# The channel MLP's beta as an extra matmul column and a relu bias, with the first batch's loads in another order

## The chip, the cores and the metric

The kernel runs on one core of a Trainium2 chip. The metric is the time of one execution in microseconds of the device (us); the time before is the median of 11 runs. Beside it there is one profiled execution, from which all durations below come.

## The reference

Grouped attention over 8 batches is followed by an MLP block over tokens and channels, with affine scalings in place of normalisations:

```python
# q: (8, 16, 384, 64), k and v: (8, 4, 384, 64); each K/V head serves 4 Q heads
scores = q @ k.T / 8
attn = softmax(scores) @ v                 # per head
x = attn.transpose(0, 2, 1, 3).reshape(8, 384, 1024)

a1 = alpha1 * x + beta1
tok = einsum('ts,bsd->btd', w_tok, a1)     # mixes tokens, w_tok: (384, 384)
u = x + lam * tok
a2 = alpha2 * u + beta2
ch = maximum(a2 @ w_ch1, 0) @ w_ch2        # w_ch1: (1024, 4096), w_ch2: (4096, 1024)
out = u + lam * ch
```

Inputs and output are float32. The kernel multiplies in bfloat16 and adds in float32.

## The kernel before, in words

The work of a batch has two parts. `side(b)` is a list of small units that make the attention and the token mixing of batch b, and end in `a2T`, the transposed input of the channel MLP. `main(b)` is the channel MLP of batch b. The program does `side(0)` alone, and then for each b runs `main(b)` with the units of `side(b + 1)` put between its matmuls at an even pace. The order on every engine is the order in which the program is written (`manual_schedule`): no engine takes a later instruction ahead of a waiting one.

`side(b)` goes by pairs of heads, p = 0 to 7, of 128 channels each. K and Q are transposed on TensorE for the first two batches (`k_transpose`, `q_transpose`, a group of two pairs each, through one PSUM buffer `tp`) and by DMA later. `scores(p, sk)` makes two matmuls and one ScalarE exp, `av_piece(p, hh)` the attention's values for one head of the pair. When the second head is done, VectorE divides by the softmax's sum (lines 207 and 210), multiplies by `g1`, which holds alpha1 times lam (L213, `a1f`), and `h1` (beta1 times lam) is added (L216): on GpSimd in the first batch for p < 6, and on VectorE otherwise. `tok(p)` mixes tokens by nine matmuls (L223, one PSUM buffer in batch 0), adds x (L226), multiplies by `al2` (L228, `a2f`) and adds `be2` (L231), again on GpSimd for p < 6 of batch 0. `a2_transpose(p)` brings a2 into `a2T`, in batch 0 by DMA from the SP queue for p < 5 and by TensorE and ScalarE for the last three. There are three buffers of a2, so that pair 7 takes that of pair 4 after its transpose has landed.

`main(b)` first runs 32 blocks of eight matmuls against W1 (L327, 384 columns each), with two PSUM buffers `mm` in turn. ScalarE takes relu of the even blocks (L332), VectorE that of the odd ones (L334). W1 does not stay in SBUF: a tile of 512 KB (two blocks) is loaded for each of 16 chunks in every batch, from GpSimd's queue, which also casts to bfloat16, into a ring of `RING = 4` buffers. A new load is issued after the matmuls that free its buffer. Then come six blocks of 32 matmuls against W2 (L347), which is loaded once, in pieces, during batch 0.

The loads of the first batch are issued ahead of `side(0)`. SP's queue carries K of batches 0 and 1 (`load_k`, two halves each, two buffers `kst`) and the broadcasts of `g1`, `lam`, `h1` (columns from 256 on), `al2` and `be2`; ScalarE's queue carries the Q of the first four heads and the broadcasts of columns 0 to 255; GpSimd's queue carries the rest of Q, V (three loads), `w_tok`, four W1 tiles, and, at places of the unit list that the table `loads` gives, half of W2 and then Q and V of batch 1. `place_k(b, i)` casts a half of K, one copy on VectorE and one on ScalarE. The pair of heads 2 and 3 (`place_k(0, 1)`) is cast ahead of the units, and its transposes stand in pair 1.

Of the kernel before, what the change touches and what calls it, by code (L numbers as in the profile page):

```python
# [12 lines left out]
def kernel(  # L13
# [21 lines left out]
    nc = tc.nc  # L35
    f32 = mybir.dt.float32
# [19 lines left out]
    NCH = NNT // CW  # L56
    RING = 4
    scale_qk = 1.0 / float(D) ** 0.5
# [9 lines left out]
    hT = const.tile([P, NNT, S], bf, tag="hT", name="hT")  # L68
    g1, h1, lam_t, al2, be2 = (const.tile([P, DM], f32, tag=n, name=n)
                               for n in ("g1", "h1", "lam", "al2", "be2"))  # L70
    kT = const.tile([P, NST, Hkv, P], bf, tag="kT", name="kT")
# [16 lines left out]
    def place_k(b, i):  # L88
        if i == 0:
            k2s[b] = sb.tile([P, NST, Hkv, 2, D], bf, tag="k2", name="k2", bufs=1)  # L90
        copies = (nc.vector.tensor_copy, nc.scalar.copy) if b < 2 else [nc.gpsimd.tensor_copy] * 2
        for a in range(2):
            copies[a](out=k2s[b][:, :, 2 * i:2 * i + 2, a, :], in_=ks[b][i].rearrange("p h st d -> p st h d"))
# [41 lines left out]

    xs, a2Ts = {}, {}

    def side(b):
        vb = vt[b % 2]
        x = sb.tile([P, NST, DM], f32, tag="x", name="x", bufs=2)  # L140
        xs[b] = x
        a2Ts[b] = sb.tile([P, NDT, S], bf, tag="a2T", name="a2T", bufs=2)
        ess, avs, a1s, a2s = {}, {}, {}, {}
# [74 lines left out]
        def tok(p):  # L218
            ps = psum.tile([P, NST, P], f32, tag="av" if first else "sc", name="tok",
                           bufs=1 if first else 2)  # L220
            for tt in range(NST):
                for st in range(NST):
                    nc.tensor.matmul(out=ps[:, tt, :], lhsT=wtokT[:, st, tt * P:(tt + 1) * P],  # L223
                                     rhs=a1s[p][:, st, :], start=(st == 0), stop=(st == NST - 1))
            u = x[:, :, cols(p)]
            nc.vector.tensor_tensor(out=u, in0=ps, in1=u, op=ADD)  # L226
            t = sb.tile([P, NST, P], f32, tag="tmp", name="a2f", bufs=4)
            nc.vector.tensor_tensor(out=t, in0=u, in1=bc(al2, p), op=MUL)  # L228
            a2s[p] = sb.tile([P, NST, P], bf, tag="a2", name="a2", bufs=3)
            eng = nc.gpsimd if first and p < NP - 2 else nc.vector  # L230
            eng.tensor_tensor(out=a2s[p], in0=t, in1=bc(be2, p), op=ADD)  # L231

        def a2_transpose(p):
            if not pe_flip or first and p < NP - 3:
                nc.sync.dma_start_transpose(
                    out=a2Ts[b][:, p, :].rearrange("p (a s) -> p a s", a=NST),
                    in_=a2s[p].rearrange("p a d -> p (a d)"))
                return
            ps = tp_ps([P, NST, P])
            for tt in range(NST):  # L240
                nc.tensor.matmul(out=ps[:, tt, :], lhsT=a2s[p][:, tt, :], rhs=ident,
                                 is_transpose=True, start=(tt == 0), stop=(tt == NST - 1),
                                 skip_group_check=True)
            nc.scalar.copy(out=a2Ts[b][:, p, :], in_=ps.rearrange("p a b -> p (a b)"))

# [44 lines left out]
        for p in range(NP):  # L290
            add(scores, p, 0)
            if p == 1:
                add(k_transpose, 2)
            add(scores, p, 1)
            if p < 3:
                add(q_transpose, p + 1)
            if p > 0:
                add(av_piece, p - 1, 0)
            if p == 2:
                add(wtok_transpose)  # L300
            if p > 2:
                add(tok_flip if p < NP - 1 else tok, p - 3)
            add(scores, p, 2)
            if p > 0:
                add(av_piece, p - 1, 1)
        for p in range(NP - 3, NP):
            if p == NP - 2:
                add(av_piece, NP - 1, 0)
                add(av_piece, NP - 1, 1)
            add(tok, p)  # L310
        for p in range(NP - 4, NP):
            add(a2_transpose, p)
        return us
# [4 lines left out]
    def main(b):  # L318
        a2T = a2Ts.pop(b)
        x = xs.pop(b)  # L320
        for c in range(NCH):
            w1 = w1_tiles.pop(b * NCH + c)
            for j in range(CW):
                nt = c * CW + j
                ps = psum.tile([P, 512], f32, tag="mm", name="h", bufs=2)
                for dt in range(NDT):
                    nc.tensor.matmul(out=ps[:, :S], lhsT=w1[:, dt, j * P:(j + 1) * P],  # L327
                                     rhs=a2T[:, dt, :], start=(dt == 0), stop=(dt == NDT - 1))
                    if dt == 3:
                        yield T_H  # L330
                if nt % 2 == 0:
                    nc.scalar.activation(out=hT[:, nt, :], in_=ps[:, :S], func=RELU)  # L332
                else:
                    nc.vector.tensor_scalar_max(out=hT[:, nt, :], in0=ps[:, :S], scalar1=0.0)  # L334
                yield T_H
# [24 lines left out]
    with tc.manual_schedule(engines=order):  # L360
# [6 lines left out]
        load_k(0)  # L367
        qst = sb.tile([P, NST, DM], f32, tag="x", name="qst", bufs=2)
        qst = qst[:, 0, :G * NST * D].rearrange("p (h st d) -> p h st d", h=G, st=NST)
        nc.scalar.dma_start(out=qst, in_=q[0, :G].rearrange("h (p st) d -> p h st d", st=NST))  # L370
        load_q(0, range(1), G)
        make_identity(nc, ident)
        for t in vt:
            nc.vector.memset(t[:, :, :, D:], 1.0)
        load_q(0, range(1, NST), G)
# [78 lines left out]
```

The softmax here doesn't subtract the row's maximum and nothing guards it: scores larger than these inputs give would overflow.

## Time and the profile before

| | us |
|---|---|
| median of 11 runs (lowest, highest) | 837.83 (834.91, 841.7) |
| profiled execution, its own time | 840.0 |
| span of the profile | 838.2 |
| TensorE busy (share of the span) | 805.5 (96%) |
| VectorE busy | 372.2 (44%) |
| ScalarE busy | 213.2 (25%) |
| GpSimd busy | 195.5 (23%) |
| W1 matmuls L327, 2048 of 327 ns | 362.4 |
| W2 matmuls L347, 1485 of 379 ns | 346.3 |
| first W1 matmul starts at | 54.59 |
| first W2 matmul starts at | 114.32 |
| batch 7's W1 part starts at | 746.66 |

Matmuls are pipelined, so the time of one is longer than the distance to the next: eight W1 matmuls take about 1.31 us when they follow each other. The page gives busy time by engine and by 40 slices of the span; the timeline gives each engine's instructions in order, and in brackets the idle time ahead of one with what ended it. "DMA q_raw<-in_q_dram" there means that the engine waited for that load. The chain of waits follows the work that ended last back from the end of the program.

### The profile page before, as it was taken

How to read it: one execution, taken by the hardware profiler on the slowest of the kernel's cores; microseconds unless marked ns; L12 is line 12 of the kernel's file. 1: busy time of each engine (PE TensorE's matmuls, PEld its weight loads, DVE VectorE, ACT ScalarE, POOL GpSimd, SP SyncE). 2: the span in 40 equal slices, each digit the busy share in tenths (PEclk: the TensorE clock that was granted, in tenths of full speed). 3: DMA queues.
4: the chain of work that ended last, by engine and by line, in shares of the span. 5: the costliest groups of instructions: out<-in, count | busy, mean ns of one | idle time of the engine just before them, and what ended most of it. 6: DMA issues, size and time to landing. Idle time of an engine off the chain costs nothing.

```text
span 838.2 us, 13671 instructions
## 1 busy us (share of the span) xinstructions
PE 805.5 (96%) x5768; PEld 436.7 (52%) x5819; DVE 372.2 (44%) x751; ACT 213.2 (25%) x337; POOL 195.5 (23%) x237
## 2 busy tenths in 40 slices
PE   5769999999999999999999999999999999999997
PEld 3545654455455654556545564556545565455443
DVE  3864653145463435534454453534455344542111
ACT  3515420232203332043212332033320432101100
POOL 5624451023301250022400223012500221003000
PEclk9979999999999999999999999999999999999999
DMA  9999999799948999499917999489994999139711
GB/s 215 214 109 173 200 204 200 141 171 179 117 90 137 173 180 79 96 170 176 155 47 147 166 179 124 89 129 171 183 86 97 144 180 124 35 70 179 101 38 38
DMA packets 265501, 115.39 MB, mean 138 GB/s; under 512 B 114272, under 2 KB 258528, under 8 KB 265440
## 3 DMA queue, kind: packets, MB, share of 16 engines
q0 software_dynamic: 202416, 83.47, 88.4%
q1 hardware_dynamic: 62064, 30.26, 15.7%
q10 hardware_dynamic: 960, 0.79, 0.4%
q8 instruction: 45, 0.74, 0.3%
q14 instruction: 16, 0.13, 0.0%
HBM read 173.08 MB, written 12.58 MB: 221 GB/s over the span
## 4 chain that ended last, share of the span: by engine, by line
PE 90%; DMA 3%; DVE 3%; issue 2%; POOL 1%; ACT 1%; DVEq 0%; POOLq 0%; ACTq 0%
PE ch L347 40%; PE h L327 38%; PE sc L179 4%; PE av L197 4%; PE tok L223 3%; DMA v<-in_v_dram 1%; DMA w<-in_moe_w_ch_dram 1%; DMA a2T<-a 1%; DVE a2f L228 1%; POOL w L125 1%; DVE x L210 0%; DVE a1f L213 0%; ACT hT L332 0%; DVE x L226 0%; PE tp L167 0%
## 5 line engine op out<-in xcount | busy, mean ns | idle before, releaser
L327 PE MATMUL h<-a2T,w 128*128 128x384 bf16 x2048 | 362.4, 327 | 3.5 <-DMA w<-in_moe_w_ch_dram 2.7
L347 PE MATMUL ch<-w,hT 128*128 128x512 bf16 x1485 | 346.3, 379 | 2.7
L327 PEld LDWEIGHTS <-w 128*128 128x128 bf16 x2048 | 190.0, 98 | 138.0 <-issue 20.4
L125 POOL DMA_DIRECT2D w<-in_moe_w_ch_dram x128 | 112.4, 879 | 558.3 <-PE sc L179 274.3
L347 PEld LDWEIGHTS <-hT 128*128 128x128 bf16 x1536 | 143.1, 98 | 162.0 <-issue 7.6
L182 ACT ACTIVATE es<-sc 128x768 bf16<-128x768 f32 x192 | 145.2, 808 | 318.8 <-PE sc L179 318.8
L334 DVE TENSOR_SCALAR hT<-h 128x384 bf16<-128x384 f32 x128 | 71.1, 555 | 165.3 <-PE h L327 165.2
L332 ACT ACTIVATE hT<-h 128x384 bf16<-128x384 f32 x128 | 62.9, 492 | 211.9 <-PE h L327 211.9
L352 DVE TENSOR_TENSOR o<-ch,lam 128x512 f32<-128x512 f32 x48 | 33.1, 689 | 127.0 <-PE ch L347 127.0
L226 DVE TENSOR_TENSOR x<-tok,x 128x384 f32<-128x384 f32 x64 | 35.6, 556 | 84.1 <-PE tok L223 84.1
L197 PEld LDWEIGHTS <-es 128*128 128x128 bf16 x1152 | 52.6, 99 | 25.5 <-issue 5.5
L197 PE MATMUL av<-v,es 128*128 128x65 bf16 x1152 | 57.7, 196 | 2.6 <-DMA v<-in_v_dram 2.6
L179 PE MATMUL sc<-qT,kT 64*128 64x384 bf16 x384 | 51.6, 340 | 1.6 <-ACT es L182 0.9
L223 PE MATMUL tok<-a,wtokT 128*128 128x128 bf16 x576 | 44.1, 223 | 9.0 <-DVE x L226 5.1
L223 PEld LDWEIGHTS <-wtokT 128*128 128x128 bf16 x576 | 38.5, 100 | 20.6 <-issue 7.9
L210 DVE TENSOR_TENSOR x<-av,rinv 128x192 f32<-128x192 f32 x128 | 39.8, 352 | 2.2
L228 DVE TENSOR_TENSOR a2f<-x,al 128x384 f32<-128x384 f32 x64 | 38.2, 598 | 2.6
L213 DVE TENSOR_TENSOR a1f<-x,g 128x384 f32<-128x384 f32 x64 | 37.6, 587 | 2.6
L207 DVE RECIPROCAL rinv<-av 128x6 f32<-128x6 f32 x64 | 12.2, 191 | 55.5 <-PE av L197 55.5
L353 DVE TENSOR_TENSOR o<-o,x 128x512 f32<-128x512 f32 x48 | 33.2, 692 | 1.6
L231 DVE TENSOR_TENSOR a<-a2f,be 128x384 bf16<-128x384 f32 x58 | 32.3, 558 | 2.8 <-DMA a2T<-a 0.8
L216 DVE TENSOR_TENSOR a<-a1f,h 128x384 bf16<-128x384 f32 x58 | 32.5, 561 | 2.0
(37 smaller groups left out, 147.8 us busy)
## 6 DMA issues: line engine op xcount, KB each, us to landing
w<-in_moe_w_ch_dram POOLq DMA_DIRECT2D x135, 512.0 KB, 6.6
out_dram<-o SPq DMA_DIRECT2D x48, 256.0 KB, 2.1
q_raw<-in_q_dram POOLq DMA_DIRECT2D x21, 256.0 KB, 8.9
kst<-in_k_dram SPq DMA_DIRECT2D x16, 192.0 KB, 3.0
w<-in_moe_w_ch_dram POOLq DMA_DIRECT2D x10, 256.0 KB, 8.9
w<-in_moe_w_ch_dram POOLq DMA_DIRECT2D x1, 2048.0 KB, 32.7
v<-in_v_dram POOLq DMA_DIRECT2D x24, 64.0 KB, 8.8
a2T<-a SPq DMA_TRANSPOSE x53, 5.1
```

The lines of the kernel that those rows point to most:

```text
L125: nc.gpsimd.dma_start(out=t, in_=w1src[:, :, c * CW * P:(c + 1) * CW * P])
L179: nc.tensor.matmul(out=sc[:, hh, :S].rearrange("p (st s) -> p st s", st=NST), lhsT=kT[r, sk, hk, :], rhs=qT[r, :, p, :], start=True, stop= ...
L182: nc.scalar.activation(out=e, in_=sc[:, :, :S], func=EXP, scale=scale_qk)
L197: nc.tensor.matmul(out=av[:, hh, sq, :], lhsT=ess[p, sk][:, hh, sq * P:(sq + 1) * P], rhs=vb[:, sk, hk, :], start=(sk == 0), stop=(sk == N ...
L210: nc.vector.tensor_tensor(out=x[:, :, c0:c0 + D], in0=av[:, hh, :, :D], in1=rinv[:, hh].to_broadcast([P, NST, D]), op=MUL)
L213: nc.vector.tensor_tensor(out=t, in0=x[:, :, cols(p)], in1=bc(g1, p), op=MUL)
L223: nc.tensor.matmul(out=ps[:, tt, :], lhsT=wtokT[:, st, tt * P:(tt + 1) * P], rhs=a1s[p][:, st, :], start=(st == 0), stop=(st == NST - 1))
L228: nc.vector.tensor_tensor(out=t, in0=u, in1=bc(al2, p), op=MUL)
L327: nc.tensor.matmul(out=ps[:, :S], lhsT=w1[:, dt, j * P:(j + 1) * P], rhs=a2T[:, dt, :], start=(dt == 0), stop=(dt == NDT - 1))
L332: nc.scalar.activation(out=hT[:, nt, :], in_=ps[:, :S], func=RELU)
L334: nc.vector.tensor_scalar_max(out=hT[:, nt, :], in0=ps[:, :S], scalar1=0.0)
L347: nc.tensor.matmul(out=ps, lhsT=hT[:, nt, ms * P:(ms + 1) * P], rhs=w2[:, nt, cs], start=(nt == 0), stop=(nt == NNT - 1))
```

## The change

Four things are changed.

1. The addition of beta2 goes. a2 is now alpha2 times u alone, one VectorE instruction. Since W1 is linear, the missing term is one number for each of W1's 4096 columns, the product of beta2 and W1. It comes as a 385th column of the right side in batch 0's W1 matmuls: beta2 is loaded as 128 x 8 single numbers and copied into column 384 of `a2T`. After each of the 32 blocks of batch 0 VectorE copies that column's result to `bias1`, and relu takes it as a bias, in all batches. `a2T` becomes two fixed tiles, and `w_tok` is loaded into a part of the tile `stage` that x uses later.
2. The loads of batch 0 are in another order. V comes as float32 from SP's queue, behind the first two halves of K, and GpSimd casts it. K of batch 1 stands ahead of the broadcasts. The broadcast of beta2 is gone.
3. In the unit list `k_transpose(2)` and `q_transpose(1)` to `(3)` stand one pair later, `place_k(0, 1)` is done after the first three scores with both copies on VectorE, and at the end the last a2 transposes stand between the last tok units. Loads of W2 and of batch 1's Q and V stand at other places of the list.
4. `RING` is 5.

```diff
-    RING = 4
+    RING = 5
...
+    bias1 = const.tile([P, NNT], f32, tag="bias1", name="bias1")
+    a2Ts = [const.tile([P, NDT, S + 16 * (1 - i)], bf, tag=f"a2T{i}", name=f"a2T{i}") for i in range(2)]
...
-        copies = (nc.vector.tensor_copy, nc.scalar.copy) if b < 2 else [nc.gpsimd.tensor_copy] * 2
+        copies = (nc.vector.tensor_copy, nc.vector.tensor_copy if i else nc.scalar.copy) if b < 2 else [nc.gpsimd.tensor_copy] * 2
...
-            t = sb.tile([P, NST, P], f32, tag="tmp", name="a2f", bufs=4)
-            nc.vector.tensor_tensor(out=t, in0=u, in1=bc(al2, p), op=MUL)
             a2s[p] = sb.tile([P, NST, P], bf, tag="a2", name="a2", bufs=3)
-            eng = nc.gpsimd if first and p < NP - 2 else nc.vector
-            eng.tensor_tensor(out=a2s[p], in0=t, in1=bc(be2, p), op=ADD)
+            nc.vector.tensor_tensor(out=a2s[p], in0=u, in1=bc(al2, p), op=MUL)
...
             add(scores, p, 0)
-            if p == 1:
+            if p == 2:
                 add(k_transpose, 2)
             add(scores, p, 1)
-            if p < 3:
-                add(q_transpose, p + 1)
+            if 0 < p < 4:
+                add(q_transpose, p)
...
-        for p in range(NP - 3, NP):
-            if p == NP - 2:
-                add(av_piece, NP - 1, 0)
-                add(av_piece, NP - 1, 1)
-            add(tok, p)
-        for p in range(NP - 4, NP):
-            add(a2_transpose, p)
+        add(tok, NP - 3)
+        add(a2_transpose, NP - 4)
+        add(av_piece, NP - 1, 0)
+        add(av_piece, NP - 1, 1)
+        add(tok, NP - 2)
+        add(a2_transpose, NP - 3)
+        add(tok, NP - 1)
+        add(a2_transpose, NP - 2)
+        add(a2_transpose, NP - 1)
...
+        n = S + 1 if b == 0 else S
...
-                    nc.tensor.matmul(out=ps[:, :S], lhsT=w1[:, dt, j * P:(j + 1) * P],
-                                     rhs=a2T[:, dt, :], start=(dt == 0), stop=(dt == NDT - 1))
+                    nc.tensor.matmul(out=ps[:, :n], lhsT=w1[:, dt, j * P:(j + 1) * P],
+                                     rhs=a2T[:, dt, :n], start=(dt == 0), stop=(dt == NDT - 1))
...
+                c1 = bias1[:, nt:nt + 1]
+                if b == 0:
+                    nc.vector.tensor_copy(out=c1, in_=ps[:, S:n])
                 if nt % 2 == 0:
-                    nc.scalar.activation(out=hT[:, nt, :], in_=ps[:, :S], func=RELU)
+                    nc.scalar.activation(out=hT[:, nt, :], in_=ps[:, :S], func=RELU, bias=c1)
                 else:
-                    nc.vector.tensor_scalar_max(out=hT[:, nt, :], in0=ps[:, :S], scalar1=0.0)
+                    nc.vector.tensor_scalar(out=hT[:, nt, :], in0=ps[:, :S], scalar1=c1,
+                                            scalar2=0.0, op0=ADD, op1=mybir.AluOpType.max)
...
+        vst = stage[:, 2, :Hkv * NST * D].rearrange("p (h st d) -> p h st d", h=Hkv, st=NST)
+        nc.sync.dma_start(out=vst, in_=v[0].rearrange("h (p st) d -> p h st d", st=NST))
+        nc.gpsimd.tensor_copy(out=vt[0][:, :, :, :D], in_=vst.rearrange("p h st d -> p st h d"))
         place_k(0, 0)
...
+        load_k(1)
         for t, ap in ((g1, moe_alpha1), (lam_t, moe_lam), (h1, moe_beta1)):
             bcast(nc.scalar, t, ap, 0, 256)
-        place_k(0, 1)
-        load_k(1)
-        for t, ap in ((g1, moe_alpha1), (lam_t, moe_lam), (h1, moe_beta1)):
             bcast(nc.sync, t, ap, 256, DM)
         bcast(nc.sync, al2, moe_alpha2, 0, DM)
-        bcast(nc.sync, be2, moe_beta2, 0, DM)
-        load_v(0)
-        wtok_in = sb.tile([P, NST, S], bf, tag="a2T", name="wtok_in", bufs=2)
+        wtok_in = stage[:, 1, :NST * S // 2].bitcast(bf).rearrange("p (tt s) -> p tt s", tt=NST)
         nc.gpsimd.dma_start(out=wtok_in, in_=moe_w_tok.rearrange("(p tt) s -> p tt s", tt=NST))
+        be2 = stage[:, 0, DM - NDT:]
+        with nc.allow_non_contiguous_dma(reason="one small vector, once"):
+            nc.sync.dma_start(out=be2, in_=moe_beta2.rearrange("(dt di) -> di dt", di=P))
         for c in range(RING):
             load_w1(c)
-        loads = {8: [(load_w2, 0, 0, 2)], 19: [(load_q, 1, [0]), (load_q, 1, [1])],
-                 25: [(load_q, 1, [2]), (load_v, 1, [0])], 37: [(load_v, 1, [1])], 43: [(load_v, 1, [2])]}
+        loads = {7: [(load_w2, 0, 0, 2)], 25: [(load_q, 1, [0]), (load_q, 1, [1])],
+                 31: [(load_q, 1, [2]), (load_v, 1, [0])], 37: [(load_v, 1, [1])], 43: [(load_v, 1, [2])]}
         for i, f in enumerate(side(0)):
             f()
...
+            if i == 4:
+                place_k(0, 1)
+        nc.vector.tensor_copy(out=a2Ts[0][:, :, S:S + 1], in_=be2[:, :, None])
         place_k(1, 0)
         place_k(1, 1)
```

More of the change, by code (lines that the diff above doesn't have):

```diff
@@ L68 @@
     hT = const.tile([P, NNT, S], bf, tag="hT", name="hT")
-    g1, h1, lam_t, al2, be2 = (const.tile([P, DM], f32, tag=n, name=n)
-                               for n in ("g1", "h1", "lam", "al2", "be2"))
+    g1, h1, lam_t, al2 = (const.tile([P, DM], f32, tag=n, name=n) for n in ("g1", "h1", "lam", "al2"))
+    bias1 = const.tile([P, NNT], f32, tag="bias1", name="bias1")
+    a2Ts = [const.tile([P, NDT, S + 16 * (1 - i)], bf, tag=f"a2T{i}", name=f"a2T{i}") for i in range(2)]
     kT = const.tile([P, NST, Hkv, P], bf, tag="kT", name="kT")
@@ L133, in tp_ps @@
         return psum.tile(shape, bf, tag="tp", name="tp", bufs=1)
-    xs, a2Ts = {}, {}
+    xs = {}
     def side(b):
@@ L141, in side @@
         xs[b] = x
-        a2Ts[b] = sb.tile([P, NDT, S], bf, tag="a2T", name="a2T", bufs=2)
+        a2T = a2Ts[b % 2]
         ess, avs, a1s, a2s = {}, {}, {}, {}
@@ L235, in a2_transpose @@
                 nc.sync.dma_start_transpose(
-                    out=a2Ts[b][:, p, :].rearrange("p (a s) -> p a s", a=NST),
+                    out=a2T[:, p, :S].rearrange("p (a s) -> p a s", a=NST),
                     in_=a2s[p].rearrange("p a d -> p (a d)"))
@@ L243, in a2_transpose @@
                                  skip_group_check=True)
-            nc.scalar.copy(out=a2Ts[b][:, p, :], in_=ps.rearrange("p a b -> p (a b)"))
+            nc.scalar.copy(out=a2T[:, p, :S], in_=ps.rearrange("p a b -> p (a b)"))
         def wtok_transpose():
@@ L318, in main @@
     def main(b):
-        a2T = a2Ts.pop(b)
+        a2T = a2Ts[b % 2]
         x = xs.pop(b)
+        n = S + 1 if b == 0 else S
         for c in range(NCH):
@@ L367 @@
         load_k(0)
-        qst = sb.tile([P, NST, DM], f32, tag="x", name="qst", bufs=2)
-        qst = qst[:, 0, :G * NST * D].rearrange("p (h st d) -> p h st d", h=G, st=NST)
+        stage = sb.tile([P, NST, DM], f32, tag="x", name="stage", bufs=2)
+        qst = stage[:, 0, :G * NST * D].rearrange("p (h st d) -> p h st d", h=G, st=NST)
         nc.scalar.dma_start(out=qst, in_=q[0, :G].rearrange("h (p st) d -> p h st d", st=NST))
-        load_q(0, range(1), G)
+        load_q(0, [0], G)
         make_identity(nc, ident)
@@ L374 @@
             nc.vector.memset(t[:, :, :, D:], 1.0)
-        load_q(0, range(1, NST), G)
+        load_q(0, [1, 2], G)
+        vst = stage[:, 2, :Hkv * NST * D].rearrange("p (h st d) -> p h st d", h=Hkv, st=NST)
+        nc.sync.dma_start(out=vst, in_=v[0].rearrange("h (p st) d -> p h st d", st=NST))
+        nc.gpsimd.tensor_copy(out=vt[0][:, :, :, :D], in_=vst.rearrange("p h st d -> p st h d"))
         place_k(0, 0)
```

## The prediction

> **What bounds the kernel now.** I read the page's row of slices first: TensorE (PE) is nine tenths busy or more in all slices but the first three and the last, while the DMA row is full in the first seven.
>
> ```profile
> PE   5769999999999999999999999999999999999997
> DMA  9999999799948999499917999489994999139711
> ```
>
> So time can be won where PE is not full. Windows over the start say how much is there: 34.35 us busy of 56, so 21.7 us idle, against about 0.5 us in each 100 us from 200 to 700 us (99.48, 99.34, 99.48, 99.48, 99.43 busy).
>
> ```profile
> 0.00:12.00 12.00, 5.92 (x29) 2.85 (x30) 3.70 (x8) 4.33 (x6) 9.27 (x16) 1.00 1.35 167
> 12.00:24.00 12.00, 8.16 (x70) 5.20 (x69) 4.99 (x12) 4.64 (x6) 3.02 (x3) 1.00 1.17 283
> 24.00:34.00 10.00, 7.92 (x102) 5.01 (x99) 8.71 (x17) 6.75 (x9) 6.54 (x6) 1.00 1.42 200
> 34.00:46.00 12.00, 7.66 (x106) 5.25 (x105) 11.16 (x21) 5.35 (x7) 9.63 (x11) 0.86 1.68 184
> 46.00:56.00 10.00, 4.69 (x32) 3.42 (x32) 7.59 (x17) 2.12 (x5) 0.99 (x1) 0.57 1.95 99
> ```
>
> After the first field come span, then busy PE, weight load, VectorE (DVE), ScalarE (ACT), GpSimd (POOL). From 24 us on DVE is the fullest engine. The PE timeline names what each gap waited for:
>
> ```profile
> 11.89 0.61 PE L167 MATMUL tp<-ident,q_raw 128*128 128x128 bf16 x4 [2.06 <-DMA q_raw<-in_q_dram]
> 18.14 0.54 PE L197 MATMUL av<-v,es 128*128 128x65 bf16 x7 [2.57 <-DMA v<-in_v_dram]
> 33.45 0.66 PE L223 MATMUL tok<-a,wtokT 128*128 128x128 bf16 x9 [0.98 <-POOL a L216]
> 47.34 1.07 PE L223 MATMUL tok<-a,wtokT 128*128 128x128 bf16 x9 [2.47 <-DVE x L226]
> 54.30 0.50 PE L241 MATMUL tp<-ident,a 128*128 128x128 bf16 x3 [1.27 <-DVE a L231]
> ```
>
> First loads (q, then v), then the DVE/POOL loop, then the tail. The timeline of those two engines shows why the loop is slow: a DVE multiply of 0.56 us lasts 1.78 us where it meets a POOL add, and the last a2 waits for a DMA.
>
> ```profile
> 35.87 1.78 DVE L228 TENSOR_TENSOR a2f<-x,al 128x384 f32<-128x384 f32 x1
> 36.24 0.99 POOL L216 TENSOR_TENSOR a<-a1f,h 128x384 bf16<-128x384 f32 x1
> 53.68 0.56 DVE L231 TENSOR_TENSOR a<-a2f,be 128x384 bf16<-128x384 f32 x1 [0.83 <-DMA a2T<-a]
> ```
>
> The chain of waits has the matching pieces: V's load, and the DMA transpose of a2 for pair 4, whose landing frees the buffer that the last a2 needs.
>
> ```profile
> 6.44 11.66 DMA v<-in_v_dram
> 45.83 7.78 DMA a2T<-a
> ```
>
> Last, batch 7, which has no attention to mix in, outruns its W1 loads (1.14 + 0.16 + 0.20 + 1.16 = 2.66 us):
>
> ```profile
> 766.16 10.77 PE L327 MATMUL h<-a2T,w 128*128 128x384 bf16 x64 [1.14 <-DMA w<-in_moe_w_ch_dram]
> 789.25 2.77 PE L327 MATMUL h<-a2T,w 128*128 128x384 bf16 x16 [1.16 <-DMA w<-in_moe_w_ch_dram]
> ```
>
> **The change part by part.**
>
> *Loads of the first batch.* (A landing here is an issue's start plus the time to landing that the DMA view gives.) V leaves POOL's software queue, where it sat behind q and landed at 18.1, and comes as f32 from SP's queue behind two K loads. Q's like-sized load took 4.6 us, so V lands at about 7; POOL casts it at its 128x384 cast's 0.51 us twice, done by about 8.5. POOL issues wtok only after that (9 instead of 7.2), but its queue is full with q until 11.9, so wtok still lands near 15 instead of 20.7. What waits: SP's second load of K(1) now needs the K cast that DVE does after its first qT copy (near 9.7), and the broadcasts of g, lam, h, al queue behind it on SP: issued from 10.2 instead of 7.7. Their landing then took 10.2 to 12 us under a load that is now smaller; h lands by about 21 to 23. DVE needs it then, so this is even, with no slack.
>
> *First transposes moved.* q_transpose(1) no longer stands before the third scores, so ACT's 2.24 us idle there goes; PE meets it after five scores, near 12, when q (11.9) is in. The attention-values step then has its V. DVE does the K cast of heads 2 and 3 alone (two of 0.5 us) while it would idle until that qT copy (idle 3.9 us before it now).
>
> From here the chain: values of pair 0 end near 13.5, DVE's normalisation (0.20 + 0.62 + 0.56 with gaps, 1.5) and the two copies for k and q (1.1) to 16.5, wtok's three transposes and copies (2.3 us, as now), and scores(2,2) near 19.5 to 20.4 instead of 24.18. From that to the first tok addition on DVE took 5.06 us; the moved qT copy adds up to 0.5. So it stands near 25.2 instead of 29.24: 4.0 us won (3 to 4.7).
>
> *The beta addition.* In the loop DVE's additions after tok stand at 29.24, 32.15, 35.23, 39.07, 42.38: 3.28 us a pair. POOL's a2 add goes (6 of 1.0 us), its a1 add stays and still meets the a2 multiply. The pair from 39.07 gives the price: addition 0.65, multiply stretched to 0.98, reciprocal and two divisions 0.86, a1f 0.62 unstretched: 3.1. I take 3.05, 12.2 for four instead of 13.14: 0.9 won. The multiply now writes a2 itself, so its transpose starts 1.63 us after the addition instead of 3.4 (42.38 to 45.8): another 1.8. But that transpose lands 7.9 us later, and then come DVE's last a2, PE and ACT, 0.99 to the first W1 matmul: 25.2 + 12.2 + 1.63 + 7.9 + 1.0 = 47.9 instead of 54.59. Without that DMA the tail's own work would end near 47.5 (3.65 + 3.2 + 1.5 for the last pairs, then a2 and PE 1.75), so it is late next. Won: 6.7; the landings of 7.1 to 8.8 and the earlier steps make 5 to 8. Re-ordered tail transposes ride in gaps: nothing.
>
> *Queue behind it.* One more W1 tile (2.6 us, from the landings at 27.4 and 30.0) now stands ahead of W2's half and q(1); V's three software loads (6.2 us under contention) are gone from it. q(1) landed at 53.8 and PE needs it 6.57 us after the first W1 matmul. By order of the queue it lands near 50, by counting all bytes as one busy system near 55; at 47.9 + 6.6 = 54.5 that is none or 0.8 us of waiting. I take 0.5 off: 6.2 won.
>
> *Beta as 1,024 single floats.* It replaces a 512 KB broadcast. The hardware queue's row on the page gives 62,064 packets in 15.7% of 16 engines' span, 34 ns each, the software queue's 59 ns: 64 packets an engine are 2.2 to 3.8 us. Against it speaks the Trainium skill, "DMA: Bandwidth & Descriptors", sections "Specifications" and "Latency and other measured facts": a strided last dimension is one descriptor an element, and one under 512 B is read, modified and written. Its own small-transfer table prices a packet at some 10.5 ns, an estimate of 0.7 us here. The broadcast moved at 350 GB/s is 1.5 us. By the row the engines lose 0.7 to 2.3 us near 13 us, by the table they gain 0.8; I take the row, as it has this chip's contention in it. The consumer is a DVE copy near 47 us, so only q(1) behind it feels it, and the 0.5 above holds it; the sum by the table would be 0.3 us better.
>
> *Bias in batch 0.* 256 matmuls get column 385. A 512-column one starts every 216.3 ns, 0.42 ns a column, and 65 columns (odd too) take 30 ns, 2.5 more than that: 0.1 to 0.6 us; I take 0.1. 32 DVE copies of 128x1 lie between the memset's 68 ns and the PSUM reciprocal's 191: at the latter 6.1 us, against 8 a2 additions dropped there (4.5). The wait is what counts: ACT's relu of even blocks now stands behind DVE's queue, and behind ACT stand the exps that scores wait for. DVE's burst of about 2 us (rinv to a1) is what odd blocks already sit through: at 105.94 to 107.90 it ran, relu ended 108.45, and the PE block that needs the buffer began 108.94. An even block there would end 0.2 us later, still in time. I take 0.3 us for all, between 0 and 4 (a quarter us at half of the blocks). The pointer operand of DVE's relu: nothing between 0.555 and 0.556 (the two-input row). In batches 1 to 7 a2 loses 0.56 us a pair on a DVE that is 45% busy: hidden by PE, nothing.
>
> *Ring of 5.* In batch 7 one more tile lies ready, so each load is needed one tile, 2.6 us, later. The waits of 2.66 are back to about 0.5 at the end where loads run at 2.85 us (512 KB at 184 GB/s) against 2.62 used: 2.2 won (1 to 2.7).
>
> Sum: -6.2 - 2.2 + 0.1 + 0.3 = -8.0. The profiled execution took 840.0 (span 838.2 and 1.8 around it), so 832.0; it stands 2.2 over the median of 11 runs, 837.83, which becomes 829.8.
>
> **The rivals.** *DMA holds the start (0.21).* For: the DMA row is full to 55 us, broadcasts are issued 2.5 us later, a transpose took up to 8.8 us, and q(1) may land at 57. Against: V's packets and a broadcast are gone. With q(1) at 57 the gain is 61.16 - 57 = 4.2 less early losses of 1.5: 2.7, and with 1.5 of the ring 833.6.
>
> *Relu's wait becomes the bound (0.10), slower.* Place: the two PSUM buffers of h in batch 0, 32 blocks. ACT's relu waits for DVE's copy, DVE for PE's tok, PE for the buffer. It decides from 8.3 / 32 = 0.26 us lost a block; at 0.5 it is 16 - 8.3, so 845.5. Against: the 0.49 us of slack at 108.45.
>
> *The start saves nothing (0.05).* If h's broadcast came 4 us later than I think, DVE would stand as now and q(1) with it; with a ring that gains 1: 837.
>
> **How the numbers follow.** The first case has 0.64, 829.8, and by its own bounds 827 to 832.5. Two in ten outside: 826.5 to 835.5 takes in the DMA case. A difference within 0.2% (1.7 us) is about what a measurement of this kernel cannot tell from none. Faster 0.64 + 0.21 = 0.85, same 0.05, slower 0.10.
>
> **What would show it.** Right: no wait of values on V; scores(2,2) near 20; POOL without L231; pairs at 3.05 us; first W1 matmul near 48 and the first q of batch 1 transposed near 54.5; no more than 0.5 us on w in batch 7; batch 0's W1 part as long as now, 59.7 us from 54.6 to 114.3. Wrong: DVE waiting for g or h near 22; PE waiting for q_raw near 55; h matmuls of batch 0 waiting for ACT.

## The result and the profile after

| | before | after |
|---|---|---|
| median, us (lowest, highest; runs) | 838.06 (834.51, 841.7; 47) | 833.97 (831.94, 834.86; 12) |
| profiled execution, its own time | 840.0 | 833.08 |
| span of the profile | 838.2 | 831.3 |
| first W1 matmul starts at | 54.59 | 50.29 |
| first W2 matmul starts at | 114.32 | 110.04 |
| batch 7's W1 part | 746.66 to 791.86 | 743.41 to 785.01 |
| VectorE / ScalarE / GpSimd busy | 372.2 / 213.2 / 195.5 | 351.1 / 224.0 / 187.8 |

The ratio of the times is 0.9949, with an interval of 0.9937 to 0.9961. The kernel is faster by 4.1 us by medians, about half of the 8.0 that was forecast. Between the two profiled executions it is 6.9 us, because before's stood 1.9 us over the median of its 47 runs and after's stands 0.9 us under its own. The clock times of the table divide these 6.9 us: 4.3 won ahead of the first W1 matmul, nothing in batch 0's W1 part (59.7 us in both), 1.0 lost from the first W2 matmul to batch 7 (632.34 to 633.37), and 3.6 won in batch 7's W1 part (45.20 to 41.60).

The page's slices of after, TensorE and DMA: only the third digit of PE has grown at the start (6 to 7), and DMA is still full in the first seven.

```profile
PE   5779999999999999999999999999999999999997
DMA  9999999799959996499917999389995999119711
```

The same windows over the start as before (span, then busy PE, weight load, DVE, ACT, POOL, then granted clock, DMA share, GB/s):

```profile
0.00:12.00 12.00, 6.39 (x33) 2.69 (x33) 4.31 (x9) 5.93 (x8) 8.52 (x15) 0.84 1.29 193
12.00:24.00 12.00, 7.09 (x73) 4.59 (x73) 5.14 (x14) 3.25 (x4) 3.20 (x4) 0.64 1.29 262
24.00:34.00 10.00, 8.30 (x116) 5.51 (x115) 9.56 (x20) 7.54 (x11) 4.68 (x5) 0.93 1.44 197
34.00:46.00 12.00, 6.27 (x92) 4.87 (x92) 10.58 (x25) 4.12 (x6) 5.93 (x7) 0.85 1.29 180
46.00:56.00 10.00, 7.62 (x47) 4.68 (x47) 4.64 (x14) 2.19 (x5) 0.89 (x1) 0.67 3.07 155
```

From 12 to 24 us, where the forecast put its largest gain, TensorE is less busy than before (7.09 us against 8.16). The granted clock of this window is lower too, 0.64 against 1.00, but TensorE's instructions in it took no longer: a pair of scores 0.50 us in both, nine matmuls of attention values 0.67 to 0.70. The timeline of TensorE names the reason, and it also shows batch 7 running through all its 256 W1 matmuls with no wait for `w`:

```profile
15.13 0.61 PE L168 MATMUL tp<-ident,q_raw 128*128 128x128 bf16 x4 [3.96 <-DMA q_raw<-in_q_dram]
...
22.38 0.50 PE L180 MATMUL sc<-qT,kT 64*128 64x384 bf16 x2
...
50.29 5.24 PE L328 MATMUL h<-a2T,w 128*128 128x385 bf16 x24
...
743.41 41.76 PE L328 MATMUL h<-a2T,w 128*128 128x384 bf16 x256
```

Nothing waits for V now, but the third load of q takes its place: it landed at 11.89 before and lands at 15.1 now, and TensorE stands 3.96 us for it, where before it stood 2.06 for q and 2.57 for V. The first addition behind tok on VectorE, which the forecast wanted at 25.2, before and after:

```profile
29.24 0.54 DVE L226 TENSOR_TENSOR x<-tok,x 128x384 f32<-128x384 f32 x1
...
27.66 0.55 DVE L227 TENSOR_TENSOR x<-tok,x 128x384 f32<-128x384 f32 x1
```

The chain of waits starts with that load of q and ends the start with the same kind of DMA transpose as before (start, length):

```profile
3.99 11.09 DMA q_raw<-in_q_dram
31.76 8.76 DMA a2T<-a
41.20 8.09 DMA a2T<-a
```

The chain's first DMA line is no longer V but q, and a second transpose has joined it: a2 of a later pair waits for the buffer of an earlier one. On VectorE this can be read three times, for pairs 4, 6 and 7:

```profile
40.62 0.56 DVE L229 TENSOR_TENSOR a<-x,al 128x384 bf16<-128x384 f32 x1 [0.66 <-DMA a2T<-a]
...
47.99 0.56 DVE L229 TENSOR_TENSOR a<-x,al 128x384 bf16<-128x384 f32 x1 [1.18 <-DMA a2T<-a]
...
49.38 0.56 DVE L229 TENSOR_TENSOR a<-x,al 128x384 bf16<-128x384 f32 x1 [0.37 <-DMA a2T<-a]
```

The loss of 1.0 us in the middle is in the groups of the page. First the two relus of before, then the W1 matmuls and the two relus of after (busy us, mean ns, idle before):

```profile
L334 DVE TENSOR_SCALAR hT<-h 128x384 bf16<-128x384 f32 x128 | 71.1, 555 | 165.3 <-PE h L327 165.2
L332 ACT ACTIVATE hT<-h 128x384 bf16<-128x384 f32 x128 | 62.9, 492 | 211.9 <-PE h L327 211.9
```

```profile
L328 PE MATMUL h<-a2T,w 128*128 128x384 bf16 (+1 forms) x2048 | 361.9, 327 | 1.5 <-ACT hT L336 1.4
...
L338 DVE TENSOR_SCALAR hT<-h,bias 128x384 bf16<-128x384 f32 x128 | 78.9, 616 | 160.5 <-PE h L328 159.7
L336 ACT ACTIVATE hT<-h,bias 128x384 bf16<-128x384 f32 x128 | 74.5, 582 | 204.2 <-PE h L328 188.6
```

A relu with a bias out of SBUF takes 90 ns longer on ScalarE and 61 ns longer on VectorE, and TensorE's h matmuls now wait 1.4 us in all for ScalarE's relu: once in each of batches 1 to 6, 0.24 us each time.

### The profile page after: what moved, and what is told of

Its sections match the earlier page's. It is cut to its first block, busy times and chain, and to the rows that moved or that the text cites. A ratio compares the mean times of both kernels' runs of the same rounds, so it can differ in the third digit from the quotient of the medians.

```text
span 831.3 us, 13628 instructions
## 1 busy us (share of the span) xinstructions
PE 802.1 (96%) x5768; PEld 435.2 (52%) x5819; DVE 351.1 (42%) x728; ACT 224.0 (27%) x335; POOL 187.8 (23%) x229
## 4 chain that ended last, share of the span: by engine, by line
PE 93%; DMA 3%; DVE 1%; issue 1%; ACT 0%; POOL 0%; DVEq 0%; POOLq 0%
PE h L328 41%; PE ch L352 40%; PE sc L180 4%; PE av L198 4%; PE tok L224 3%; DMA a2T<-a 2%; DMA q_raw<-in_q_dram 1%; ACT hT L336 0%; PE tp L168 0%; DVE a L229 0%; PE tp L239 0%; DVE x L211 0%; PE tp L249 0%; DVE a1f L214 0%; POOL q_raw L104 0%
## 5 line engine op out<-in xcount | busy, mean ns | idle before, releaser
L328 PE MATMUL h<-a2T,w 128*128 128x384 bf16 (+1 forms) x2048 | 361.9, 327 | 1.5 <-ACT hT L336 1.4
L338 DVE TENSOR_SCALAR hT<-h,bias 128x384 bf16<-128x384 f32 x128 | 78.9, 616 | 160.5 <-PE h L328 159.7
L336 ACT ACTIVATE hT<-h,bias 128x384 bf16<-128x384 f32 x128 | 74.5, 582 | 204.2 <-PE h L328 188.6
L198 PEld LDWEIGHTS <-es 128*128 128x128 bf16 x1152 | 52.1, 98 | 22.2 <-issue 2.2
L229 DVE TENSOR_TENSOR a<-x,al 128x384 bf16<-128x384 f32 x64 | 37.7, 589 | 4.3 <-DMA a2T<-a 2.2
L214 DVE TENSOR_TENSOR a1f<-x,g 128x384 f32<-128x384 f32 x64 | 35.7, 558 | 2.4
L180 PEld LDWEIGHTS <-kT 64*128 64x128 bf16 x384 | 12.2, 94 | 36.1 <-issue 34.9
```

The costliest lines, as they stand in the source:

```text
L180: nc.tensor.matmul(out=sc[:, hh, :S].rearrange("p (st s) -> p st s", st=NST), lhsT=kT[r, sk, hk, :], rhs=qT[r, :, p, :], start=True, stop= ...
L198: nc.tensor.matmul(out=av[:, hh, sq, :], lhsT=ess[p, sk][:, hh, sq * P:(sq + 1) * P], rhs=vb[:, sk, hk, :], start=(sk == 0), stop=(sk == N ...
L214: nc.vector.tensor_tensor(out=t, in0=x[:, :, cols(p)], in1=bc(g1, p), op=MUL)
L229: nc.vector.tensor_tensor(out=a2s[p], in0=u, in1=bc(al2, p), op=MUL)
L328: nc.tensor.matmul(out=ps[:, :n], lhsT=w1[:, dt, j * P:(j + 1) * P], rhs=a2T[:, dt, :n], start=(dt == 0), stop=(dt == NDT - 1))
L338: nc.vector.tensor_scalar(out=hT[:, nt, :], in0=ps[:, :S], scalar1=c1, scalar2=0.0, op0=ADD, op1=mybir.AluOpType.max)
```

## The experiments

Times are given as median (lowest to highest) and the ratio to the kernel before on the same chip, whose medians were 837.39, 837.51 and 836.07 us in the three groups: the first four experiments, the next four, the last two. The changed kernel's own 833.97 (ratio 0.9949) stands beside a before of 838.06, so a difference of medians can have some of the difference between groups in it; where it matters, the difference of the ratios is given too. All edits are to the changed kernel unless it is said otherwise.

### A ring of 4

```diff
-    RING = 5
+    RING = 4
```

> The changed kernel with RING = 4 again, nothing else. Theory A (the two profiles add up: the start gave 4.3 us, the ring 3.6 in batch 7, the bias operand of relu costs 1.0): first W1 matmul near 50.3 as in the changed kernel, W1 waits of 2 to 3 us in batch 7, and 3 to 3.6 us slower than the changed kernel, so 0.5 to 1 us faster than before. Theory B (the start gave nearly all, since W1's loads now meet less traffic): within 1 us of the changed kernel.

836.87 us (835.87 to 839.34), ratio 1.0000 [0.9990, 1.0011]. With a ring of 4 the whole rest of the change is worth nothing that can be measured. Batch 7 has its waits again:

```profile
765.39 18.76 PE L328 MATMUL h<-a2T,w 128*128 128x384 bf16 x112 [1.43 <-DMA w<-in_moe_w_ch_dram]
...
784.45 5.43 PE L328 MATMUL h<-a2T,w 128*128 128x384 bf16 x32 [0.30 <-DMA w<-in_moe_w_ch_dram]
```

Its W1 part took 44.11 us against 41.60, with 1.73 us of waits, less than the 2 to 3 that were expected. The fifth buffer is worth 2.9 us by the medians (836.87 less 833.97), the larger part of the gain, and 4.3 by the ratios (0.0051).

### The old start with beta and the ring

Loads, unit order and casts of the first batch as before; beta's column, the bias and the ring of 5 stay.

```diff
-        vst = stage[:, 2, :Hkv * NST * D].rearrange("p (h st d) -> p h st d", h=Hkv, st=NST)
-        nc.sync.dma_start(out=vst, in_=v[0].rearrange("h (p st) d -> p h st d", st=NST))
-        nc.gpsimd.tensor_copy(out=vt[0][:, :, :, :D], in_=vst.rearrange("p h st d -> p st h d"))
...
+        load_v(0)
...
-            if 0 < p < 4:
-                add(q_transpose, p)
+            if p < 3:
+                add(q_transpose, p + 1)
...
```

> Beta as a column and the ring of 5 as in the changed kernel, but the first batch's loads, their order, the unit order and the casts as before (V on GpSimd's queue). Theory A: beta alone wins what the loop won, since GpSimd's second addition is gone (2.5 to 3 us by the first W1 matmul), and the new order only the other 1.5; so first W1 matmul at 51.5 to 52.5, and 1 to 2 us slower than the changed kernel. Theory B, the new order carries the start: first W1 matmul at 54 to 54.6 and 3.5 to 4.3 us slower than the changed kernel.

833.64 us (833.23 to 834.64), ratio 0.9956 [0.9943, 0.9970]: the same as the whole change. TensorE waits for V as the old order did,

```profile
17.79 0.54 PE L198 MATMUL av<-v,es 128*128 128x65 bf16 x7 [3.35 <-DMA v<-in_v_dram]
```

and the first W1 matmul stands at 51.03, 0.74 us behind that of the changed kernel, which does not show in the medians. Neither theory of the expectation holds, since both had this version slower. The new order of loads wins nothing measurable.

### Beta alone

The edit above and the ring of 4 together: what is left of the change is the column and the bias.

```diff
-    RING = 5
+    RING = 4
...
-            if p == 2:
+            if p == 1:
...
```

> Beta as a column alone: the start as before and RING = 4. Theory A: first W1 matmul at 51.5 to 52.5, waits in batch 7 as before, relu's operand costs 1.0: 1 to 2 us faster than before. Theory B: no faster than before, or slower by the 1.0 of relu's operand.

835.82 us (832.57 to 838.3), ratio 0.9983 [0.9972, 0.9993]: 1.6 us won by beta's change alone. Against the ring of 4 with the new loads (836.87) it is even 1.05 us better; against the old start with a ring of 5 (833.64) it is 2.2 us worse, which is a second measure of the ring. The spread is wide, 5.7 us, and the profiled execution was one of the quickest (832.93): it has no wait for V, and its first W1 matmul stands at 47.55, where theory A had 51.5 to 52.5 and the same start with a ring of 5 had 51.03. So its clock times are not those of its median.

### V back in the software queue

V comes by three loads of GpSimd's queue behind q, without a cast; everything else as in the changed kernel.

```diff
-        vst = stage[:, 2, :Hkv * NST * D].rearrange("p (h st d) -> p h st d", h=Hkv, st=NST)
-        nc.sync.dma_start(out=vst, in_=v[0].rearrange("h (p st) d -> p h st d", st=NST))
-        nc.gpsimd.tensor_copy(out=vt[0][:, :, :, :D], in_=vst.rearrange("p h st d -> p st h d"))
...
+        load_v(0)
```

> The changed kernel, but V of batch 0 comes in three loads of GpSimd's queue again, behind q and ahead of w_tok, without GpSimd's cast. Theory A (V's load on SP's queue takes DMA time from q, whose third load landed at 15.1 instead of 11.9): q's third load lands near 12 again, PE's wait on q is about 1 us instead of 4, but it waits for V at 17 to 18 instead; first W1 matmul later than 50.3 by 1 to 2 us. Theory C (q is late for another reason, the earlier K loads or broadcasts): q lands near 15 all the same and V near 20, first W1 matmul 3 us or more later.

833.94 us (833.57 to 834.38), ratio 0.9957 [0.9944, 0.9970]: no difference. The wait for q is gone, and one for V is back:

```profile
14.53 0.22 PE L198 MATMUL av<-v,es 128*128 128x65 bf16 x1 [2.03 <-DMA v<-in_v_dram]
14.90 0.55 PE L198 MATMUL av<-v,es 128*128 128x65 bf16 x7 [0.16 <-DMA v<-in_v_dram]
```

Everything but V's way is the same here, so the 384 KB of V on SP's queue are what delays q in the changed kernel. (GpSimd's cast of V starts at 7.34 us there, after the last load of q was issued at 3.99.) The other profiles agree: TensorE gets q at 14.6 to 15.6 us in the five versions that have V on SP's queue and q as in the changed kernel, and at 10.5 to 12.1 in the four profiles of the old order. Whichever of the two loads goes first, the other is in at about 15 us. V is in near 14.9; the four profiles of the old order have it in between 15.5 and 18.1, so it is open whether the other moved loads gave it anything. The loss that theory A put on V's return did not come: the first W1 matmul stands at 49.62, 0.67 us earlier than in the changed kernel.

### q's second transpose later

```diff
-            if 0 < p < 4:
+            if 1 < p < 4:
...
+            if p == 1:
+                add(q_transpose, 1)
```

(The second place is behind the attention values of pair 0.)

> The changed kernel, with q_transpose(1) in TensorE's order behind the values of pair 0 instead of ahead of them (both only need to be done before pair 2's scores). Theory D (in the changed kernel the new order only swaps the wait for V for a wait for q: with V at 7.3 but q's third load at 15.1, everything behind q_transpose(1) stands): values of pair 0 and its division are made at 11 to 14 instead of 15.5 to 18.8, DVE is free when q comes, first W1 matmul 1 to 2 us earlier than 50.3 and the median 0.5 to 2 us below the changed kernel's. Theory E (the start is held by the later DMAs, broadcasts, w_tok or transposes, whatever PE does first): first W1 matmul within 0.5 us.

833.71 us (832.46 to 835.04), ratio 0.9956 [0.9939, 0.9973]: no gain by the measure. TensorE's wait for q falls from 3.96 to 1.17 us, but VectorE's next work now meets the broadcasts:

```profile
13.08 0.42 DVE L204 TENSOR_TENSOR g<-g,lam 128x256 f32<-128x256 f32 x1 [4.20 <-DMA lam<-in_moe_lam_dram]
14.15 0.42 DVE L205 TENSOR_TENSOR h<-h,lam 128x256 f32<-128x256 f32 x1 [0.65 <-DMA h<-in_moe_beta_dram]
```

VectorE copies q's transposes at 15.85 in the end, where it did at 15.77 in the changed kernel. The first tok addition moves from 27.66 to 27.36 only, and the first W1 matmul to 49.54, between the two theories. Program order cannot win back what the DMA engines have not yet brought; the loads behind q are late as well.

### The transposes of pairs 3 and 4 on TensorE

```diff
-            if not pe_flip or first and p < NP - 3:
+            if not pe_flip or first and p < NP - 5:
...
-                add(tok_flip if p < NP - 1 else tok, p - 3)
+                add(tok_flip if p < NP - 2 else tok, p - 3)
+            if p == NP - 1:
+                add(a2_transpose, 3)
```

> The changed kernel, with the a2 of pairs 3 and 4 of batch 0 transposed by TensorE and ScalarE, so that only pairs 0 to 2 go by DMA. Theory: in the changed kernel DVE waits 0.66, 1.18 and 0.37 us for a2 buffers whose DMA transposes take 8 to 10 us to land, and the first W1 matmul stands 1.0 us behind the last landing. Without it the DVE chain ends the start: first W1 matmul near 48.1, 2.2 us earlier, median 1.5 to 2.2 below the changed kernel's. Rival: PE's own in-order waits for a2 in the loop cost as much as is won: within 0.5 us.

833.48 us (832.42 to 834.15), ratio 0.9950 [0.9932, 0.9967]. VectorE's three waits for a2's buffers (2.21 us) become one of 0.45, and the first W1 matmul comes at 48.98 instead of 50.29. Of these 1.3 us 0.4 were there already at the first tok addition (27.23 against 27.66), which the edit does not touch. The medians show 0.5, which these runs cannot tell from none: by them, the expectation's rival.

### The relu without its bias in batches 1 to 7

The kernel leaves beta's term out of these seven batches, so that their relu has the form of before.

```diff
-                    nc.scalar.activation(out=hT[:, nt, :], in_=ps[:, :S], func=RELU, bias=c1)
+                    nc.scalar.activation(out=hT[:, nt, :], in_=ps[:, :S], func=RELU, **({'bias': c1} if b == 0 else {}))
...
+                    else:
+                        nc.vector.tensor_scalar_max(out=hT[:, nt, :], in0=ps[:, :S], scalar1=0.0)
```

> The changed kernel, with relu in batches 1 to 7 as before (no bias operand, so the beta term is left out of these batches); batch 0 is as changed. Theory F (the bias operand makes ScalarE's relu 0.58 us instead of 0.49, which costs PE's PSUM rotation some 1.0 us over batches 1 to 7): L336 at 0.49 us there, PE's waits on ACT hT gone (1.4 us in the changed kernel), from first W1 matmul to batch 7's W1 part 692.1 us instead of 693.1, and 0.7 to 1.2 us faster. Rival: the difference of 1.0 between the two traces is in batch 0 (385th column, waits for the bias copies): it stays, same time within 0.3 us.

832.38 us (830.85 to 833.27), ratio 0.9936 [0.9912, 0.9960]. The groups by form, ScalarE's relu and the W1 matmuls of these batches:

```profile
L336 ACT ACTIVATE hT<-h 128x384 bf16<-128x384 f32 x112 | 55.0, 491 | 194.4 <-PE h L328 194.4
...
L328 PE MATMUL h<-a2T,w 128*128 128x384 bf16 x1792 | 311.4, 326 | 0.9
```

The relu is at 491 ns again, no W1 matmul is put down to waiting for it, and the stretch from the first W2 matmul (111.3) to batch 7 (743.60) is 632.3 us, as in the kernel before and 1.0 us shorter than in the changed kernel. Seven of the other eight versions, all with the bias, took 633.36 to 633.39 us there, and the eighth, beta alone, 633.88. By medians the bias costs 1.6 us, by ratios 1.1, with runs that overlap. The profiled execution itself, 833.27, is no quicker than the changed kernel's (833.08): its first 24 W1 matmuls took 6.63 us instead of 5.24, for a reason given at the end.

### A third of q staged as float32

Heads 4 to 7 of q, a third of what the software queue brought, come as float32 by ScalarE's hardware queue, into the tile that hT uses later, and two VectorE copies cast them. GpSimd's software queue brings three loads of 128 KB instead of 192.

```diff
-        load_q(0, [0], G)
+        nc.scalar.dma_start(out=qst2, in_=q[0, G:2 * G].rearrange("h (p st) d -> p h st d", st=NST))
+        load_q(0, [0], 2 * G)
...
-        load_q(0, [1, 2], G)
+        load_q(0, [1, 2], 2 * G)
...
+                for h in (0, 2):
+                    nc.vector.tensor_copy(out=qrs[0][:, :, G + h:G + h + 2, :],
+                                          in_=qst2[:, h:h + 2].rearrange("p h st d -> p st h d"))
```

> The changed kernel, with q of heads 4 to 7 loaded as float32 from ScalarE's queue too (into hT, which is unused until the channel MLP), cast by two VectorE copies behind the K casts; GpSimd's queue carries heads 8 to 15 alone. Theory D (q's many short packets in the software queue are what PE waits for): PE's wait of 4 us at q_transpose(1) is gone or under 1 us, values of pair 0 near 11.5, first W1 matmul 2 to 3.5 us earlier than 50.3, median 1.5 to 3 us below the changed kernel's. Theory E: the wait turns into one for w_tok, g or h of like length, first W1 matmul within 0.7 us.

830.97 us (830.63 to 831.72), ratio 0.9923 [0.9896, 0.9949]: 3.0 us under the changed kernel, with no overlap of their runs; by the ratios it is 2.2, and 2.1 between the two profiled executions. There is no wait for q. What is late next is `w_tok`, by little, the first tok addition is at 24.58 instead of 27.66, and the first W1 matmul stands 3.15 us earlier (the last line is VectorE's tok addition):

```profile
17.01 0.50 PE L249 MATMUL tp<-ident,stage 128*128 128x128 bf16 x3 [0.61 <-DMA stage<-in_moe_w_tok_dram]
...
47.14 6.01 PE L328 MATMUL h<-a2T,w 128*128 128x385 bf16 x24
...
24.58 0.55 DVE L227 TENSOR_TENSOR x<-tok,x 128x384 f32<-128x384 f32 x1
```

The bytes read from memory are the same, and only the share that goes through the casting queue is smaller. So the hold was not the sum of the bytes read, but the way that q takes. One thing is not told apart: heads 4 to 7 go by another queue, and they also no longer come in one load with heads 8 to 15. The third load of these was in only near 12.9 us (issued near 3.7, 9.2 to landing), after TensorE had begun on heads 4 to 7 at 11.27. Loading heads 4 to 7 first in the software queue was not tried.

### Both of the last edits that moved the start

q staged, and the transposes of pairs 3 and 4 on TensorE: the two diffs above together, of which this is the second.

```diff
-            if not pe_flip or first and p < NP - 3:
+            if not pe_flip or first and p < NP - 5:
...
```

> Both that helped: q of heads 4 to 7 staged as float32 (as in the run that staged it) and the a2 of pairs 3 and 4 transposed by TensorE. Theory: in the run with q staged alone the tail still waited 0.39, 0.19 and 0.68 us for a2 buffers and stood 1 us behind the last landing; so first W1 matmul near 46 instead of 47.1, and 0.5 to 1.2 us faster than with q staged alone (830.97). Rival: the tail's gain drowns, same within 0.5 us.

830.24 us (829.63 to 830.48), ratio 0.9928 [0.9915, 0.9941]. The first W1 matmul is at 45.99:

```profile
45.99 6.70 PE L330 MATMUL h<-a2T,w 128*128 128x385 bf16 x24
```

It has the lowest median here, 0.7 us under the one with q staged alone and 3.7 under the changed kernel. But the kernel before was 1.4 us quicker in this group too (836.07 against 837.51), and the ratio, 0.9928 against 0.9923, shows no gain over q staged alone. The two profiles do: the first W2 matmul stands at 107.20 instead of 107.96, and the executions took 830.32 and 830.98. So some 0.7 us are likely and not shown.

### The kernel before, once more

No edit: one execution, to see how much of the prediction's numbers was that one profile.

> The kernel before once more, for its trace alone. Theory G (V's landing in the old order differs from run to run, 18.1 in the trace that the prediction read, 15 or earlier in the run with beta alone): PE's wait for V differs from 2.57 us by more than 1 us, and the first W1 matmul lies between 51 and 54. Rival (the old order always costs that wait): 2.3 to 2.9 us, first W1 matmul at 54.6 within 0.5.

835.32 us, against 840.0 for the execution that the prediction read. Its timeline has the same waits at other sizes; V's is shorter by 0.55 us, less than the 1 us of theory G, whose 51 to 54 for the first W1 matmul fits:

```profile
17.07 0.54 PE L197 MATMUL av<-v,es 128*128 128x65 bf16 x7 [2.02 <-DMA v<-in_v_dram]
...
784.56 2.77 PE L327 MATMUL h<-a2T,w 128*128 128x384 bf16 x16 [0.54 <-DMA w<-in_moe_w_ch_dram]
```

The first tok addition is at 27.42 (29.24 there), the first W1 matmul at 52.15 (54.59), and batch 7 waits once, 0.54 us (four times, 2.66 us there), with a W1 part of 42.95 us (45.20). The stretch from the first W2 matmul to batch 7 is 632.3 us in both, so the start and the end of the kernel are what varies. Set against this execution, the changed kernel's profile is 2.2 us faster, by 1.9 at the start and 1.35 in batch 7, less the 1.0 in between.

## Why the prediction was half right

The forecast was 829.8 us, 8.0 less than the median of its 11 runs (837.83), with 826.5 to 835.5 as its range; 833.97 lies in it. That it is near the DMA rival's 833.6 is luck: that sum had the q of batch 1 in at 57 us and waited for, and nothing waited for it. The same steps in the order of the sum:

| step | predicted | after against the profile read | after against before once more |
|---|---|---|---|
| first tok addition | -4.0 | -1.6 | +0.2 |
| from there to the first W1 matmul | -2.7 | -2.7 | -2.1 |
| q of batch 1 | +0.5 | 0 | 0 |
| column, copies and bias in batch 0 | +0.4 | 0 | 0 |
| bias in batches 1 to 7 | 0 | +1.0 | +1.0 |
| ring, batch 7 | -2.2 | -3.6 | -1.35 |
| sum | -8.0 | -6.9 | -2.2 |

Against the profile read the sums nearly agree, but in part by luck: the first step fell 2.4 short, and the ring gave 1.4 more than its 2.2.

- **The step that failed is the one on the loads.** The prediction let V land at about 7, which it did (issued at 1.76, 5.5 us to landing), and left q's third load at 11.9. It was at 15.1. The prediction had read the DMA row as full in the first seven slices, and yet it put what the 384 KB of V, now ahead, would cost q at nothing. V back in the software queue took the wait for q away and put one for V in its place at the same time of the kernel, so one load was moved ahead at the other's cost. The second scores of pair 2, forecast at 19.5 to 20.4, stood at 22.38, and the first tok addition at 27.66 instead of 25.2. With q staged it stood at 24.58, near where the forecast wanted it: the rest of that step's chain was right.
- **The size was taken from one execution that was late in both places that the change touches.** The fresh run of before has its first tok addition 1.8 us earlier and 2.1 us less of waiting on W1 in batch 7. The sum was set against the profiled time, which was right for that execution (6.9 us came out), and then carried over to a median that seems not to have all of these waits: the fresh run is a quick one too (0.75 us under the median of its group), so those of a median run should lie between the two. Of the gain by medians only 4.1 us are left.
- **The step from the tok loop to the first W1 matmul was right as a sum.** 22.7 us forecast (47.9 less 25.2), 22.63 measured; the two executions of the kernel before took 25.35 and 24.73, so 2.1 to 2.7 were won. Within it four pairs took 11.75 us instead of 12.2, and the tail the rest, because a2 waited for transposes three times, not once. The two versions with the old start have it too (22.1 and 22.2 us), so this gain is beta's: GpSimd's second add is gone, and a2 is ready one instruction earlier.
- **The pointer operand was mis-sized.** It was priced at nothing on VectorE by a row of another form, and not priced on ScalarE at all. It takes 61 and 90 ns. The forecast's cover, the two PSUM buffers, holds in most blocks, but once in each of batches 1 to 6 TensorE waits 0.24 us for ScalarE's relu, which had started as soon as its block was done (at 198.75 in the first of them, after 2.29 us of idle time) and was only too long. Dropping the bias in seven batches gave the 1.0 us back.
- **Batch 0, for which the loss was feared, took 59.7 us, as forecast, and this was luck.** The first 24 of its W1 matmuls took 5.24 us in this profile and 5.58 in both of the kernel before; what came behind them took 54.5 instead of 54.15. So the 0.4 us of the sum were there. The other versions have 54.5 to 54.8 behind the first 24 too, and for the 24 themselves 5.16 once and 5.85 to 6.80 in the eight others.
- **The ring was right in kind and size.** 2.2 us forecast; 2.9 and 2.2 by the two pairs of medians (4.3 and 2.3 by their ratios), and no wait on `w` in batch 7. How much it won in batch 7 depends on the execution that it is set against: 3.6, 2.5 (the ring of 4) or 1.35.
- **Nothing waited for beta's 1,024 floats.** The load was issued near 13.9 and took 12.2 us to land, with its consumer near 47; the q of batch 1 was not waited for either. What these packets cost the engines is not told apart by any run here. (That a strided last dimension is one descriptor an element stands in the section "Rules for kernel authors" of the page "DMA: Bandwidth & Descriptors" of the Trainium skill, and not in either of the two that the prediction names.)
- **Split by medians:** the ring about -2.2 to -2.9, beta -1.6, net of its bias's 1.0 to 1.6, and the load order between nothing (833.97 against 833.64 with a ring of 5) and +1.05 (836.87 against 835.82 with a ring of 4). What the new order does seem to give is evenness: 11 of 14 runs with a ring of 4 lie between 836.1 and 837.2, where the old start with that ring spreads over 832.6 to 838.3. With a ring of 5 it does not show: five runs of the old start lie within 1.4 us, the changed kernel's 12 within 2.9. Why the old start varies so with a ring of 4 is open: V's last load took 9.1 to 11.7 us to land in the four profiles that have it in the old order, but what sets that was not tried.

## What to carry to other kernels

A load that is moved ahead takes its time from those it overtakes even if they are in another queue: write down, for each load of the start, when it will land after the move, not only the one whose wait is shown. If the late load is a casting one in the software queue, bring the part that is needed first as float32 by a hardware queue and cast it on an engine that idles there; here this won 3.0 us by medians and 2.1 between the profiles, where the re-ordering won none. Where a phase has no cover, one more buffer is worth its waits, and an added operand of an instruction that runs 256 times has to be priced by a row of that very form. And a sum made of waits for transfers needs more than one execution of the kernel, or a range that allows for those waits being half as long.

## What was not expected of the hardware

- A bias per partition read from SBUF lengthens a relu of 128x384 from PSUM: 492 to 582 ns on ScalarE, 555 to 616 ns on VectorE (as an add and a maximum with one pointer, against one maximum).
- A load of 384 KB on SP's queue put the third of three 192 KB casting loads of q, on GpSimd's queue, from 11.9 to 15.1 us, with 193 GB/s moved in the first 12 us.
- DMA transposes of a2, forecast to land in 7.9 us, took 8.1 and 8.8 on the chain: with three buffers they set VectorE's pace at the end of the start, even where VectorE has become faster.
- The first 24 W1 matmuls, 3.9 us at the later pace, took from 5.2 to 6.8 us by profile (5.24 after, 6.80 with the ring of 4). The granted clock accounts for it. After, it is 0.50 from 50 to 52 us and 0.84 from 52 to 54, then 1.00; with the ring of 4 it is 0.50 from 50 to 56 and 0.90 from 56 to 58. If it went from 0.50 to 1.00 once, that is some 2.3 us of W1 matmuls at half the clock in the one and 5.5 in the other, half of which is lost: an estimate of 5.1 and 6.7 us. How early the W1 part starts does not decide it: from 47.55 on the 24 took 5.16 us (beta alone), from 50.91 on 6.80. What does is not shown by these runs. Batch 0's W1 part took 59.7 us in the changed kernel and 60.8 with q staged, so this alone can hide 1 us of what a change wins in the start when single profiles are compared.
